# Transformer layer on one core: the order of instructions taken from a time table, queries in six units of 256 and four of 128 per head group

## The chip, the core and the metric

The kernel runs on one core of a Trainium2 chip. A core has five engines, each with its own queue that is worked off strictly in order: TensorE (PE in the profile; its weight loads are shown apart as PEld), VectorE (DVE), ScalarE (ACT), GpSimd (POOL) and SyncE (SP), which here only issues DMAs. Engines meet through semaphores. Matmuls write to PSUM, eight banks of 128 partitions by 512 fp32 values; DVE and ACT read them from there. The metric is the device time of one execution in microseconds (us), lower is better. The kernel before took 1297.13 us (median of three runs, 1290.29 to 1299.14).

## What is computed

A pre-norm attention block and a gated FFN over 2048 tokens of width 512, with 32 heads of 16 columns; inputs and output are bfloat16.

```python
def _A_ref(x, wqkv, wo):            # S = 2048, D = 512, H = 32, Dh = 16
    qkv = (x @ wqkv).reshape(B, S, 3, H, Dh).transpose(2, 0, 3, 1, 4)
    q, k, v = qkv[0], qkv[1], qkv[2]
    scores = jnp.einsum("bhqd,bhkd->bhqk", q, k) * (Dh ** -0.5)
    p = _softmax(scores, axis=-1)
    o = jnp.einsum("bhqk,bhkd->bhqd", p, v)
    return o.transpose(0, 2, 1, 3).reshape(B, S, D) @ wo

def _B_ref(x, w_gate, w_up, w_down):  # F = 1792
    return (_gelu(x @ w_gate) * (x @ w_up)) @ w_down

h = x + _A_ref(_layernorm(x), wqkv, wo)
h2 = h + _B_ref(_layernorm(h), w_gate, w_up, w_down)
```

## The kernel before

**Units.** Heads are taken four at a time, one to each 32-row group of the PE array ("slot": 8 of them). Queries are taken 256 at a time ("group": `gi`, 8 of them). A unit is one group and one slot, so there are 64; a slot's scores for 256 queries are 4 heads x 256 x 2048 numbers.

**Two passes over the scores.** The first pass (`p1_pair`, `p1_consume`) multiplies 128 queries of two heads by 512 keys into two PSUM banks (L653, matmuls in 32-row tiles), and DVE takes the row maxima of both banks in one reduction (L662, 128x1024 in, 128x2 out). A unit has 16 such steps (four key chunks `kc`, two query halves, two pairs of heads), the kernel 1024. GpSimd folds the maxima of the key chunks (L673 to L690), splits the result into three bfloat16 parts (L693 to L696, tile ST), SP transposes them by DMA (L702, tile STG), and GpSimd adds them to spare rows of QT (L707), so that the second pass's matmul already subtracts the maximum. The second pass (`p2_pair`, `p2_consume`) computes the transposed scores, keys on partitions (L728, two matmuls of 256 columns to a bank), and ACT takes exp of a whole bank (L741): 32 banks a unit, 2048 in all. The result goes to a ring of 34 tiles PT. `item_pv` multiplies it by V with a column of ones (L755, four heads in four 32-column tiles), so the denominators come along.

**Rounds.** A loop over ticks (L1150) writes the program. One tick has one first-pass pair, one second-pass pair of an earlier unit (the second pass runs 24 ticks behind), and one piece of "dense" work, the matmuls in whole-array form: projections, V products, output projection (`item_oproj`), gate, up and down of the FFN (`item_gate`, `item_up`, `item_down`). Where no dense piece is ready, `dummy` (L1144) issues filler matmuls of 512 columns. The waits of a tick's row-tiled matmuls are drawn together (`group_begin`, `group_end`). GpSimd's work goes through `PoolStream` with a budget of 1.19 us a tick. Evacuations go to ACT while the first pass lasts (`evac_act`), later to DVE.

```python
cost = dense.piece()
if cost and not p2_started:
    dense.piece()
if (cost or 0) < 2:
    dummy(banks.free[0], 2 - (cost or 0))
run_deferred(tick)
pool.tick()
```

**Start.** SP loads x in four chunks of 512 KB, then wqkv (1536 KB) and wo. DVE takes the statistics of all 16 tiles (L338, L339), GpSimd their rsqrt by a power (L343), DVE normalizes tiles 0 to 11 and GpSimd tiles 12 to 15 (L349); PE transposes (L354), ACT copies out (L356). `w_order` (L361) copies Q's and K's weights into another column order, so that a projection's 128 columns hold the heads of two slots: one in place, one shifted by 16 partitions by a DMA (QKS to QKS2), each then masked. K of head tile 0 for all four key chunks and Q for the first are projected before the first pass starts.

**FFN and tail.** tanh-gelu is put together from five GpSimd operations (L930 to L934) and one ACT tanh (L925). Gate and up work on two blocks of 128 FFN columns for 256 tokens (one bank). The last group's FFN runs after everything else (`tail_a`, `tail_b`), with ACT's own gelu; its layer norm takes row sums from ACT (L1105, L1107) and a chain on GpSimd (L886 to L907).

Of the kernel before, what the change touches and what calls it, by code (L numbers as in the profile page):

```python
# [1 line left out]

# [2 lines left out]

class _Eng:
    def __init__(self, name, sem):
        self.name = name
        self.sem = sem
        self.count = 0  # L10
        self.ops = []
        self.known = {}
        self.group_start = None


class Plan:

    ENGINES = ("pe", "act", "dve", "pool", "sp")

    def __init__(self, nc, es):  # L20
# [10 lines left out]
        self.n_waits = 0  # L31
        self.held = set()
        self.implied = {}

# [6 lines left out]
    def _deps(self, reads, writes):  # L41
        deps = []
        for b in reads:
# [3 lines left out]
            if b in self.held:  # L47
                raise RuntimeError("plan: read of incompletely written buffer %r" % (b,))
# [15 lines left out]
    def _waits_for(self, e, deps, extra=()):  # L64
# [17 lines left out]
        self.n_waits += len(waits)  # L82
        return waits

    def op(self, eng, fn, reads=(), writes=(), sig=True, extra_deps=()):
        e = self.eng[eng]
        deps = self._deps(reads, writes)
        waits = self._waits_for(e, deps, extra_deps)
        if sig:
            e.count += 1  # L90
            tok = (eng, e.count)
        else:
            tok = (eng, e.count + 1)
        if sig:
            self.implied[tok] = dict(e.known)
# [4 lines left out]
    def dma(self, eng, fn, semkey, reads=(), writes=(), extra_deps=()):  # L100
# [3 lines left out]
        waits = self._waits_for(e, deps, extra_deps)  # L104
        self.dma_count[semkey] += 16
        tok = (semkey, self.dma_count[semkey])
        self.implied[tok] = dict(e.known)
# [4 lines left out]
    def group_begin(self, eng):  # L112
        e = self.eng[eng]
        e.group_start = len(e.ops)
        e.group_count = e.count

    def group_end(self, eng):
        e = self.eng[eng]
        i0 = e.group_start
        e.group_start = None  # L120
        if i0 is None or i0 >= len(e.ops):
            return
        allw = []
        for i in range(i0, len(e.ops)):
            fn, waits, sig, dsem = e.ops[i]
            allw.extend(waits)
            e.ops[i] = (fn, [], sig, dsem)
        need = {}
        for (k, v) in allw:
            if k == eng and v > e.group_count:  # L130
                continue
            if v > need.get(k, 0):
                need[k] = v
        fn, _, sig, dsem = e.ops[i0]
        e.ops[i0] = (fn, sorted(need.items(), key=lambda kv: kv[0] != "act"), sig, dsem)

    def wait(self, eng, tokens):
        e = self.eng[eng]
        waits = self._waits_for(e, tokens)
        if waits:  # L140
            e.ops.append((None, waits, False, None))

    def retire(self, keys):
        toks = []
        for b in keys:
            t = self.last_writer.get(b)
            if t is not None:
                toks.append(t)
            toks.extend(self.readers.get(b, ()))
        need = {}  # L150
        for (k, v) in toks:
            if v > need.get(k, 0):
                need[k] = v
        return list(need.items())

    def finish(self, eng="sp"):
        self.wait(eng, [(k, v) for k, v in self.dma_count.items() if v > 0])

    def emit(self, block):
        nc = self.nc  # L160
# [43 lines left out]
NFC = F // 128  # L204
EPS = 1e-5
GC = 0.7978845608028654

NPT_M, NPT_E, NPT_G = 23, 4, 7
NPT = NPT_M + NPT_E + NPT_G
PV_T = (13, 14, 16, 17)  # L210
ADDX = 4
LAGX = 8
PAUSE = 1


def bass_sequential_preLN__mha_block__geglu_ffn__prompt_kernel(nc, A_x, A_wqkv, A_wo, B_x, B_w_gate, B_w_up, B_w_down, out):
    dbg = None
    with ExitStack() as es:
        block = es.enter_context(nc.Block())
        P = Plan(nc, es)  # L220

# [3 lines left out]
        arena = es.enter_context(nc.sbuf_tensor("arena", [128, ARENA // 2], BF16))  # L225
# [26 lines left out]
        wq_r = at("wq_r", [128, 4, D], BF16)  # L252
        wk_r = at("wk_r", [128, 4, D], BF16)
# [977 lines left out]
```

## Time and profile before

| | us |
|---|---|
| median of the runs | 1297.13 |
| profiled execution | 1296.73 |
| its span, first to last instruction | 1294.8 |
| DVE busy | 1198.6 (93%) |
| ACT busy | 1199.7 (93%) |
| PE busy | 1160.2 (90%) |
| POOL busy | 761.0 (59%) |
| first reduction (L662) starts | 35.3 |
| first exponential (L741) starts | 67.6 |
| last reduction ends | 1225.6 |
| last exponential ends | 1258.4 |

The profile is one execution. Busy time is the union of an engine's instructions; matmuls overlap one another, so a busy PE may still be far from full. In the profile's groups each row is a source line with its engine, output and input tiles, shapes and count, then busy time, the mean duration of one in ns, and the idle time of the engine just before, with what ended it. A duration is longer than the distance from one start to the next where an engine overlaps successive instructions; the timeline shows that distance. The granted clock is TensorE's, 1.00 being full speed; over the span its mean was 0.987.

### The profile page before, as it was taken

How to read it: one execution, taken by the hardware profiler on the slowest of the kernel's cores; microseconds unless marked ns; L12 is line 12 of the kernel's file. 1: busy time of each engine (PE TensorE's matmuls, PEld its weight loads, DVE VectorE, ACT ScalarE, POOL GpSimd, SP SyncE). 2: the span in 40 equal slices, each digit the busy share in tenths (PEclk: the TensorE clock that was granted, in tenths of full speed). 3: DMA queues.
4: the chain of work that ended last, by engine and by line, in shares of the span. 5: the costliest groups of instructions: out<-in, count | busy, mean ns of one | idle time of the engine just before them, and what ended most of it. 6: DMA issues, size and time to landing. Idle time of an engine off the chain costs nothing.

```text
span 1294.8 us, 31432 instructions
## 1 busy us (share of the span) xinstructions
PE 1160.2 (90%) x12678; PEld 445.6 (34%) x12678; DVE 1198.6 (93%) x1101; ACT 1199.7 (93%) x2440; POOL 761.0 (59%) x1534
## 2 busy tenths in 40 slices
PE   3999888899998999899999999899998999989998
PEld 2233222333333333333333333233333333333325
DVE  5899999999999999999999999999999999999802
ACT  3599999999999999999999999999999999999972
POOL 5567763387636773477635774467733876367731
PEclk9999999999999999999999999999999999999969
DMA  3110003300010000100010000100001000100000
GB/s 130 42 32 24 20 20 123 81 6 6 5 28 14 6 5 8 34 6 6 4 29 14 6 4 10 26 11 6 6 21 20 6 6 5 28 14 5 6 9 17
DMA packets 48688, 27.45 MB, mean 21 GB/s; under 512 B 34976, under 2 KB 47008, under 8 KB 48544
## 3 DMA queue, kind: packets, MB, share of 16 engines
q1 hardware_dynamic: 48544, 25.44, 7.5%
q8 instruction: 101, 1.65, 0.6%
q14 instruction: 43, 0.35, 0.1%
HBM read 11.80 MB, written 2.10 MB: 11 GB/s over the span
## 4 chain that ended last, share of the span: by engine, by line
DVE 56%; ACT 15%; POOL 15%; PE 11%; issue 2%; DMA 1%; POOLq 0%
DVE PM L662 55%; ACT PTM L741 8%; POOL LINV L790 4%; ACT PTG L741 2%; POOL th_sb L934 2%; PE pbank L728 2%; POOL th_sb L932 2%; PE pbank L1144 2%; PE pbank L942 2%; ACT th_sb L925 2%; PE pbank L653 2%; PE pbank L603 1%; ACT PTE L741 1%; PE pbank L551 1%; POOL QT L707 1%
## 5 line engine op out<-in xcount | busy, mean ns | idle before, releaser
L662 DVE TENSOR_REDUCE PM<-pbank 128x2 f32<-128x1024 f32 x1024 | 1168.4, 1216 | 34.0 <-PE pbank L728 18.2
L741 ACT ACTIVATE PTM<-pbank 128x512 bf16<-128x512 f32 x1388 | 737.9, 661 | 10.4 <-PE pbank L728 4.0
L728 PE MATMUL pbank<-QT,KT 32*128 32x256 bf16 x4096 | 514.0, 275 | 24.1 <-ACT PTM L741 12.8
L653 PE MATMUL pbank<-KT,QT 32*128 32x512 bf16 x2048 | 398.9, 385 | 28.8 <-DVE PM L662 12.8
L1144 PE MATMUL pbank<-ones_bf,ident 128*128 128x512 bf16 x822 | 256.9, 388 | 41.3 <-ACT u_sb L516 7.8
L741 ACT ACTIVATE PTG<-pbank 128x512 bf16<-128x512 f32 x420 | 228.4, 650 | 2.7 <-PE pbank L728 1.3
L653 PEld LDWEIGHTS pbank<-KT,QT 32*128 32x128 bf16 x2048 | 101.5, 91 | 374.2 <-DVE PM L662 148.8
L728 PEld LDWEIGHTS pbank<-QT,KT 32*128 32x128 bf16 x4096 | 172.3, 92 | 89.3 <-ACT PTM L741 47.9
L741 ACT ACTIVATE PTE<-pbank 128x512 bf16<-128x512 f32 x240 | 137.4, 661 | 2.3 <-PE pbank L728 1.3
L755 PE MATMUL pbank<-PTM,VA 128*17 128x256 bf16 x2776 | 126.9, 276 | 1.5
L688 POOL TENSOR_TENSOR MX<-PM,MX 128x8 f32<-128x8 f32 x64 | 12.8, 199 | 170.6 <-DVE PM L662 170.6
L1144 PEld LDWEIGHTS pbank<-ones_bf,ident 128*128 128x128 bf16 x822 | 49.5, 97 | 148.9 <-ACT PTM L741 90.3
L790 POOL TENSOR_TENSOR LINV<-OAT,negone 128x16 f32<-128x16 f32 (+1 forms) x32 | 92.7, 2896 | 11.8 <-DVE OAT L505 11.8
L677 POOL TENSOR_TENSOR MX<-PM,MX 128x8 f32<-128x8 f32 x64 | 12.9, 202 | 108.8 <-DVE PM L662 108.8
L755 PEld LDWEIGHTS pbank<-PTM,VA 128*17 128x17 bf16 x2776 | 60.6, 90 | 45.9 <-issue 29.3
L942 PE MATMUL pbank<-hnT_l,wu_sb 128*128 128x256 bf16 x448 | 69.2, 281 | 4.7 <-ACT PTG L741 0.2
L942 PE MATMUL pbank<-hnT_l,wg_sb 128*128 128x256 bf16 x448 | 67.9, 277 | 4.2 <-ACT PTM L741 0.6
L934 POOL TENSOR_TENSOR th_sb<-th_sb,g_sb 128x512 f32<-128x512 f32 x49 | 62.0, 1266 | 4.1
L707 POOL TENSOR_TENSOR QT<-QT,STG 128x256 bf16<-128x256 bf16 x64 | 42.7, 667 | 36.9 <-DMA STG<-ST 36.9
L931 POOL TENSOR_TENSOR th_sb<-th_sb,g_sb 128x512 f32<-128x512 f32 x49 | 62.0, 1266 | 2.9
L983 POOL TENSOR_TENSOR GUT<-th_sb,u_sb 128x512 bf16<-128x512 f32 x49 | 62.1, 1268 | 2.7
L990 PE MATMUL pbank<-wd_sb,GUT 128*128 128x512 bf16 x224 | 61.3, 386 | 0.5
(128 smaller groups left out, 1073.0 us busy)
## 6 DMA issues: line engine op xcount, KB each, us to landing
QKS<-QKS SPq DMA_DIRECT2D x32, 112.0 KB, 2.1
x_sb<-in_A_x_dram SPq DMA_DIRECT2D x4, 512.0 KB, 5.5
xres<-in_A_x_dram SPq DMA_DIRECT2D x16, 128.0 KB, 2.2
out_dram<-out_sb SPq DMA_DIRECT2D x16, 128.0 KB, 1.8
wg_sb<-in_B_w_gate_dram SPq DMA_DIRECT2D x4, 448.0 KB, 5.1
wu_sb<-in_B_w_up_dram SPq DMA_DIRECT2D x4, 448.0 KB, 4.9
wqkv_sb<-in_A_wqkv_dram SPq DMA_DIRECT2D x1, 1536.0 KB, 10.3
wd_sb<-in_B_w_down_dram SPq DMA_DIRECT2D x3, 512.0 KB, 6.2
```

The costliest lines, as they stand in the source:

```text
L653: P.op("pe", lambda e, g=g, b=b: e.matmul(pbank[:, b, :], QT[32 * g:32 * g + 32, c, slot, 128 * qt:128 * qt + 128], KT[32 * g:32 * g + 32, ...
L662: P.op("dve", lambda e: e.tensor_reduce(out=PM[:, par, qt, kc, g:g + 2], in_=pbank[:, b:b + 2, :], axis=AX.X, op=ALU.max), reads=[("pb", b ...
L728: P.op("pe", lambda e, g=g, b=b, kt=kt, i=i: e.matmul(pbank[:, b, 256 * i:256 * i + 256], KT[32 * g:32 * g + 32, slot, 128 * kt:128 * kt + ...
L741: P.op("act", lambda e, b=b, pi=pi: e.activation(out=PTt(pi), in_=pbank[:, b, :], func=ACT.Exp), reads=[("pb", b)], writes=[("PT", pi)], e ...
L755: P.op("pe", lambda e, g=g, kt=kt, pi=pi, i=i: e.matmul(pbank[32 * g:32 * g + 17, b, 0:256], VA[:, kt, 4 * slot + g, :], PTt(pi)[:, 256 * ...
L790: P.op("pool", lambda e: e.tensor_tensor(out=li, in0=oat4[:, :, :, 16], in1=negone[:, 0:8 * ns].rearrange("p (q h) -> p q h", q=2), op=ALU ...
L931: o(1.27, lambda e: e.tensor_tensor(out=ts_, in0=ts_, in1=gs, op=ALU.mult), [("th", par), ("g", par)])], then=done)
L934: o(1.27, lambda e: e.tensor_tensor(out=ts_, in0=ts_, in1=gs, op=ALU.mult), [("th", par), ("g", par)])], then=lambda: defer(1, lambda: lat ...
L942: P.op("pe", lambda e, dc=dc, fc=fc, i=i: e.matmul(pbank[:, b, 256 * i:256 * i + 256], w[:, dc, 128 * fc:128 * fc + 128], hT[:, dc, :], st ...
L983: P.op("pool", lambda e: e.tensor_tensor(out=o_ap, in0=shp(ts_), in1=shp(us), op=ALU.mult), reads=[("th", par), ("u", par)], writes=o_keys ...
L990: P.op("pe", lambda e: e.matmul(pbank[:, b, :], GUT[:, fc, 128 * k:128 * k + 128], wd_sb[:, fc, :], start=(fc == 0), stop=False), reads=[( ...
L1144: P.op("pe", lambda e: e.matmul(pbank[:, b, :], ident[:], ones_bf[:, 0:512], start=True, stop=True), reads=["ident", "ones_bf"], writes=[( ...
```

## The change

The whole scheduling half of the kernel is rewritten; the operations on the data stay mostly the same.

- **Groups.** 2048 queries are six groups of 256 and four of 128, so 80 units. In a 128-query unit the second pass puts four matmuls of 128 columns in a bank, gate and up put four blocks of FFN columns in a bank. There the maxima of the four key chunks are folded by one small DVE reduction (`negm_small`); in the last unit DVE does the splitting and the addition too.
- **Order.** `Plan` keeps a modelled time for every instruction. The main loop compares when the next first-pass pair, the next second-pass bank and the next dense piece could start, and writes out the one that comes first by its rules; GpSimd's jobs have priorities, extra ACT passes wait for a gap of two exponentials. There are no ticks and no grouped waits. Fillers of 256 columns are written where nothing could start within 0.35 us by the table.
- **First units.** The first-pass steps of units 0 and 1 alternate by key chunk. Only K and Q of head tile 0 for the first 512 tokens are projected ahead; the other chunks follow between the reductions. Statistics of tiles 8 to 15 are taken by two ACT passes each, and GpSimd normalizes these tiles.
- **Transfers.** The first four tiles of x are loaded one by one, then K's columns of wqkv, Q's, the rest of x, V's.
- **Weights.** Q's and K's weights are used in their own column order; V's columns are picked by `head(slot, g)`, and the transposed output is written back in the right order.
- **Tail.** The last group has 128 queries; its layer norm takes statistics straight from PSUM on DVE, in two halves.

```diff
+GROUPS = [(256 * i, 256) for i in range(6)] + [(1536 + 128 * i, 128) for i in range(4)]
...
+    def mm(self, fn, reads=(), writes=(), n=512, mode="f", tile=0, sig=False, slow=1, extra=()):
...
+        run = slow * n / 2400.0 + 0.0025
+        if mode == "f":
+            run = max(run, 0.058)
...
-        for c in range(NCH):
-            P.dma("sp", lambda e, c=c: e.dma_start(out=x_sb[:, 4 * c:4 * c + 4, :], in_=xv[:, 4 * c:4 * c + 4, :]),
-                  ("x", c), writes=[("x", c)])
-        P.dma("sp", lambda e: e.dma_start(out=wqkv_sb[:], in_=wv), "wqkv", writes=["wqkv"])
+        for t in range(4):
+            P.dma("sp", lambda e, t=t: e.dma_start(out=x_sb[:, t, :], in_=xv[:, t, :]), ("x", t), writes=[("x", t)], lat=2.4 + 0.1 * t, ivl=0.4)
+        P.dma("sp", lambda e: e.dma_start(out=wqkv_sb[:, :, D:2 * D], in_=wv[:, :, D:2 * D]), "wk", writes=["wk"], lat=3.8)
+        P.dma("sp", lambda e: e.dma_start(out=wqkv_sb[:, :, 0:D], in_=wv[:, :, 0:D]), "wq", writes=["wq"], lat=4.8)
...
+        def head(slot, g):
+            return 8 * (slot // 2) + 2 * g + slot % 2
...
+        for kc in range(4):
+            for ui in (0, 1):
+                seq += [(ui,) + s_ for s_ in steps_of(ui) if s_[0] == kc]
+        for ui in range(2, NU):
+            seq += [(ui,) + s_ for s_ in steps_of(ui)]
...
+        def negm_small(ui):
+            par = ui % 2
+            last = ui == NU - 1
+            dve(lambda e: e.tensor_reduce(out=NEGM[:, par, 0:4], in_=PM[:, par, :, 0, :].rearrange("p k g -> p g k"), axis=AX.X, op=ALU.max, negate=True),
+                [("PM", par, k_, 0, gp_) for k_ in range(4) for gp_ in range(2)], [("NEGM", par)], 0.1, 0.2)
...
+            P.dma("sp", lambda e: e.dma_start_transpose(out=STG[:, par, 0:w].rearrange("p (q s) -> p q s", q=nq), in_=ST[:, par, 0:nq].rearrange("p q s -> p (q s)")),
+                  ("stT", par), reads=[("ST", par)], writes=[("STG", par)], lat=2.35, ivl=0.1)
...
+        def pool_bank():
+            best, bt = None, INF
+            for b in (2, 3, 4, 5, 6, 7) if p1_over[0] else (4, 5, 6, 7):
...
+            for i in range(nk):
+                kt = m * nk + i
+                P.mm(lambda e, kt=kt, i=i: e.matmul(pbank[:, b, w * i:w * i + w], KT[32 * g:32 * g + 32, slot, 128 * kt:128 * kt + 128],
+                                                    QT[32 * g:32 * g + 32, c, slot, col:col + w], start=True, stop=True, tile_position=(32 * g, 0)),
...
+        def late_stats(c):
+            sl = slice(4 * c, 4 * c + 4)
+            for t in range(4 * c, 4 * c + 4):
+                for (func, dst, key) in ((ACT.Copy, hsum, "hs1"), (ACT.Square, hsq, "hq1")):
+                    def go(t=t, func=func, dst=dst, key=key):
+                        act(lambda e: e.activation(out=PTM[:, t, :], in_=x_sb[:, t, :], func=func, accum_out=dst[:, t:t + 1]), [("x", t)], [(key, t), ("PT", t)], 512, ivl=0.9, lat=1.0)
...
-            if (cost or 0) < 2:
-                dummy(banks.free[0], 2 - (cost or 0))
...
+            if P.pe_mode == "r" and best_row <= tr + 0.06:
+                kind = "row"
+            elif sd < INF and ed + 0.09 <= min(D1, D2) + 0.03 and sd <= best_row + 0.5:
+                kind = "dense"
+            elif best_row < INF and best_row <= sd + 0.3:
+                kind = "row"
+            elif sd < INF:
+                kind = "dense"
+            else:
+                kind = None
...
+            if best_row > P.pe_at("f") + 0.35:
+                b, bt = pool_bank()
+                if b is not None and bt <= P.pe_at("f") + 0.02:
+                    dummy(b, 256)
+                    continue
+            if f1 <= f2 + 0.02:
+                p1_issue()
+            else:
+                p2_issue(tl, b2)
```

## The prediction

> **What bounds the kernel now.** I first cut the span into stretches at the first reduction, the first exponential, the last reduction and the last exponential, and read the busy time of each engine there (columns: stretch, its length, busy us and instructions of each engine, granted clock, DMA):
>
> ```profile
> 0.00:35.30 35.30, 14.97 (x86) 8.73 (x86) 18.18 (x55) 14.14 (x24) 16.48 (x32) 1.00 0.36 120
> 35.30:67.60 32.30, 31.27 (x150) 9.82 (x150) 29.59 (x25) 16.24 (x30) 20.42 (x34) 1.00 0.16 46
> 67.60:1225.60 1158.00, 1052.62 (x11997) 398.92 (x11996) 1138.81 (x1000) 1135.17 (x2327) 705.78 (x1437) 1.00 0.07 18
> 1225.60:1258.40 32.80, 31.09 (x254) 9.35 (x253) 1.97 (x4) 25.83 (x50) 13.69 (x18) 0.67 0.04 11
> 1258.40:1294.80 36.40, 30.29 (x203) 18.74 (x194) 10.03 (x18) 8.27 (x15) 4.58 (x13) 0.92 0.04 15
> ```
>
> The third busy figure is DVE, the fourth ACT. Between the ends both run at 98%; before 35.30 and after 1225.60 DVE has little to do. The groups say what the 98% is, the timeline how fast a reduction can follow another:
>
> ```profile
> L662 DVE TENSOR_REDUCE PM<-pbank 128x2 f32<-128x1024 f32 x1024 | 1168.4, 1216 | 34.0 <-PE pbank L728 18.2
> L1144 PE MATMUL pbank<-ones_bf,ident 128*128 128x512 bf16 x822 | 256.9, 388 | 41.3 <-ACT u_sb L516 7.8
> ```
>
> ```profile
> 699.33 5.74 DVE L662 TENSOR_REDUCE PM<-pbank 128x2 f32<-128x1024 f32 x5
> 700.14 2.11 ACT L741 ACTIVATE PTM<-pbank 128x512 bf16<-128x512 f32 x4
> ```
>
> Five reductions in 5.74 us, the last 1.214 long: one starts every 1.131 us. Four exponentials in 2.11 us, the last 0.66: every 0.48 (0.477 between most starts in the trace). So 1024 reductions need 1023 x 1.131 + 1.214 = 1158.2 us of DVE, and 2048 exponentials 977 us of ACT, to which some 140 us of evacuations, tanh and squares come. DVE is the floor, ACT some 4% below it in issue time. The middle holds 1000 reductions in 1158.0 us, 27 us over their 1131. The chain of waits at the end:
>
> ```profile
> 1241.59 0.54 PE pbank L728 x4
> 1242.13 0.96 PE pbank L1144 x2
> 1243.10 0.54 PE pbank L728 x4
> ...
> 1269.60 0.40 PE pbank L1078 x4
> ...
> 1271.71 6.49 PE pbank L942 x48
> ```
>
> At the lower clock (0.67 in this stretch) a round for two exponentials takes 1.51 us; then come the last FFN's 256 queries. The profiled execution took 1296.73 us, 1.93 around its span, and lies 0.4 under the median of the runs.
>
> **The change, part by part.** The 1024 reductions and 2048 exponentials of the same size stay: nothing in the floor moves. All gain must come from the ends and the 27 us.
>
> *Head.* x comes first as four tiles of 128 KB. Four issues took 2.11 us, 0.53 each; a load of that size landed after 2.2 (the xres row), so tile 0 is there at 0.79 + 2.2 = 3.0, not 4.88. Statistics take 0.8 a tile (4.88 to 5.70). Then per tile: next statistics 0.8, an addition 0.16, GpSimd's power 0.58 (the rows of 128x1), normalizing 0.40, handovers: 2.0. Tile 3 ends at 3.0 + 0.8 + 3 x 2.0 + 1.2 = 11.0. Transposes 0.4, their copy 0.6, the K projection 1.0, its evacuation 0.8: 13.8, and Q's evacuation on DVE 14.8. The built order puts four normalizations (1.15 each with their powers) and two statistics ahead of the first reduction on DVE: 14.8 + 6.2 = 21. PE has 16 V-projection matmuls and eight transposes before the first pair (to about 18), which that covers; the V weights, now tenth in SP's queue, must be there by 14: before, the same 3.5 MB of x and weights had landed by 2.94 + 10.3 = 13.2, so they just are. The eight weight reorderings (0.29 each on DVE) go, since the head permutation moves into V's columns and a strided transpose output. First reduction at 21 instead of 35.3, between 18 and 26.
>
> Tiles 8 to 15 get their statistics on ACT: sixteen passes at about 0.6 each, ten us, in a stretch where ACT was busy 16 of 32 us; then eight normalizations on GpSimd at 0.77. By the built order their eighth pass stands behind about 17 us of ACT work, so chunk 2 of K comes at about 40, and the two interleaved units consume 16 reductions, 18 us, from 21 on: to 39. Chunk 3 comes at about 50, when chunk 2 is used up at 49. I take 6 us for these waits (0 to 12). Were the two units not interleaved, only 8 reductions would cover them. The first exponential stands behind 34 pairs instead of 25, at about 66, as before; ACT's 977 + 140 from there fits.
>
> *Middle.* Here the fixed rounds with two filler matmuls give way to an order written out from a time table. By the built order PE changes between its tile modes 1522 times instead of 2097 (about 0.1 us each: 58 us of PE), and 822 fillers (0.22 each: 180 us) become 230, nearly all at the ends. The lag of exponentials behind reductions stays (975 against 974 at reduction 512). The 27 us went mostly to reductions behind L728 (18.2), which waited for banks that ACT held while it waited for GpSimd's gelu; the new order emits a tanh only where its product should be there. I take half of the 27, 13.5, and keep none (0) and all (27) as ends.
>
> The last 512 queries come in units of 128: 31 small maxima on DVE at 0.1, 3 us; for a quarter of the reductions, 256, PE's score and V matmuls double in number at half the width. What a 128-column matmul costs is in the last transposes: four in 0.40 us, one 0.22 to 0.23 long by its own row, so 56 ns each, weight loads included. Per reduction PE then has 8 transposed-score matmuls, 2 rounds of four V matmuls, and 1.75 of gate and up, 11.75 x 56 = 0.66, plus 0.08 for the rest of the FFN and 0.16 for 1.6 mode changes: 0.90, and 1.12 if the first scores' 0.22 hides nowhere. That is under 1.131, but close; 3 us for it.
>
> *End.* After the last pair of scores 52 exponentials stand on ACT (before: 50): 24.8, and 2.8 for tanh and evacuations, less 2 since that pair is issued ahead of its reduction, plus 3 for PE: 28.6, against 32.8. The chain of the last unit (its maximum and splitting on DVE 0.9, SP's transpose 2.3, addition 0.25) is covered by the 20 exponentials of the unit before, 9.5. From the last exponential on, 36.4 now: the FFN of one 128-row tile is 112 x 56 + 28 x 107 = 9.3 instead of 19.5, and statistics straight from PSUM on DVE (2.5) stand in for two ACT passes and GpSimd's chain (6.6 from 1263.02). 36.4 - 10.2 - 4.1 = 22.1, and 2 less for half-width steps: 20 (17 to 26).
>
> Sum: 21 + 1158.2 + 3 + 6 + 13.5 + 3 + 28.6 + 20 + 1.9 = 1255.
>
> **Rivals.** *PE becomes the bound in the narrow units* (slower than before). 11.75 matmuls at c, 0.24 beside: DVE's 1.131 is passed at c = 75 ns if the first scores are hidden, at 57 if not. If each 128-column matmul waits for its whole weight load (92 to 98 ns by their rows, 94 taken), a reduction needs 1.35 to 1.57 of PE, 55 to 110 us over 256: 1310 to 1365. Against it is the 56 ns of the four transposes, four in a row only; for it, that such a stream stands nowhere else in the profile. The Trainium skill ("TensorE: Matmul & The Clock Gate", Back-to-back issue gap) gives about 81 ns for streams of load and matmul at N=128; by it the sum would be 1272, or 1327 with nothing hidden. The trace's 56 differs from it. Chance 0.13.
>
> *The clock falls in the middle.* The fillers were a seventh of PE's streaming time there. Without them the dense work fills 25% and both score streams 19% (all overlapped) to 57% (none). In the trace the stretches of 3.4 us before the two falls in the middle (at 752 and 1161 us) stream 45% and 38%; the leanest without a fall 44%. Exponentials free banks one by one, so the scores hardly all overlap; I expect 60 to 70%. At half clock a round costs 0.38 more (1.51 - 1.131): a fifth of the rounds, 78 us, 1333. Chance 0.05. The same page (Part 1) lets the clock fall after an idle window of about 3.4 us; by that rule there would be no fall here, but the fourth stretch above shows 0.67 with PE busy 31 of 33 us.
>
> *The written order waits.* An engine can't pass over a step that the time table had too early. The table gives SP 0.1 us for issuing a transpose; the row of L702 has 1.17, landing 2.3 to 4.1. If each of the 80 units held up PE by half a us, 40 us: 1295. Against: a unit's exponentials begin some 8 reductions, 9 us, after its last one, and the chain takes 5 to 8. Chance 0.10.
>
> *Only the ends gain, or all waits go* (1268 or 1241) are inside my case, chance 0.72; the built order shows the change doing what it says.
>
> **The numbers.** Likeliest 1255. My case with all ends low is 18 + 1158 + 3 + 0 + 0 + 3 + 27 + 17 + 2 = 1228, seldom all at once: low 1232. High 1290 takes in most of the third rival and the mild part of the first. This kernel's runs tell about 1% from no change: 1284 and 1310. Faster: 0.71 of my case, 0.04 of the first rival, 0.02 of the third: 0.77. Same: 0.01 + 0.04 + 0.05 = 0.10. Slower: 0.05 + 0.05 + 0.03 = 0.13.
>
> **What would show it.** First reduction at 18 to 26 us; reductions still 1.131 apart; DVE idle in the middle under 25 us; PE's clock 1.00 there; no denser waits of DVE for PE in the last quarter; under 24 us after the last exponential. Wrong if DVE's idle time grows after reduction 768 (first rival), if half-clock windows stand in the middle (second), or if DVE waits recur at unit starts (third).

## The result, and the profile after

The changed kernel took 1379.65 us (median of four runs, 1365.37 to 1385.21), the kernel before on the same chip 1296.04. The ratio is 1.0634, with a 95% interval of 1.0545 to 1.0723: slower by some 83 us, where 42 us less had been forecast. The profiled execution took 1379.94 us, its span 1378.2. The ratios of the experiments below leave out single runs that took longer than the others of their kernel, for a cause that isn't known: 1378.08 of a_share3000 (the profiled one, so no small difference is read from its row), 1412.33 of a_wide, 2582.0 of a_noint and 1639.63 of the kernel before.

The same cut as before, at the first reduction (23.00), the first exponential (76.20), the last reduction (1323.90) and the last exponential (1352.20). Columns again: stretch, its length, busy us and instructions of PE, PEld, DVE, ACT, POOL, granted clock, DMA share, GB/s.

```profile
0.00:23.00 23.00, 21.50 (x116) 10.16 (x117) 11.73 (x36) 11.34 (x22) 7.92 (x22) 1.00 0.61 193
23.00:76.20 53.20, 46.95 (x256) 18.34 (x253) 38.10 (x35) 28.92 (x63) 42.75 (x63) 0.90 0.09 26
76.20:1323.90 1247.70, 1180.49 (x13188) 508.08 (x13190) 1147.70 (x1022) 1135.69 (x2351) 703.07 (x1391) 0.80 0.07 17
1323.90:1352.20 28.30, 26.21 (x582) 19.56 (x570) 7.22 (x20) 27.21 (x57) 21.85 (x24) 0.94 0.05 13
1352.20:1378.20 26.00, 22.83 (x248) 17.36 (x248) 6.74 (x17) 6.38 (x13) 4.94 (x8) 0.99 0.04 11
```

Both ends are about where the forecast had them: the first reduction at 23.0 instead of 35.3, and 54.3 us from the last reduction to the end instead of 69.2. Most of the loss is in the third line (the second is 20.9 us longer, too, with 35 DVE instructions instead of 25). The third has nearly the same work for DVE and ACT as before (1148 and 1136 us, against 1139 and 1135), takes 90 us more for it, and its clock is 0.80 where it was 1.00. The row of the granted clock, one digit for a fortieth of the span, shows that this is no single event:

```profile
PEclk9899766697957889689885889778976689988879
```

Summed up from the records of the clock, of which the last ends 2 us behind the span, 507.7 us ran at half clock, in 50 separate falls of 2.6 to 27.3 us; before it was 36.5 us, most of it after the last reduction. The groups of the two score passes and of the fillers (busy us, mean ns, then the engine's idle time before them and what ended it), and what DVE waited for (total us, times, longest):

```profile
L684 DVE TENSOR_REDUCE PM<-pbank 128x2 f32<-128x1024 f32 x1024 | 1185.0, 1215 | 115.1 <-PE pbank L822 60.9 <-PE pbank L681 50.9
L681 PE MATMUL pbank<-KT,QT 32*128 32x512 bf16 x2048 | 502.3, 455 | 17.7 <-DVE PM L684 13.9
L440 PE MATMUL pbank<-ones_bf 128*128 128x256 bf16 (+1 forms) x230 | 48.4, 335 | 1.8 <-POOL ones_bf L467 1.4
```

```profile
DVE PM L684 <- PE pbank L822: 60.9, 130, 1.9
DVE PM L684 <- PE pbank L681: 50.9, 67, 5.3
```

A reduction is as long as it was (1215 ns against 1216), but 115 us of idle time stand before the reductions instead of 34, and it is PE that ends it. No single wait is long: 130 of 1.9 us or less, 67 of 5.3 or less. That is PE running a little behind DVE again and again. PE's score matmuls went from 385 ns on average to 455.

To see whether the clock and the waits belong together I put each distance between two reduction starts down to the clock it ran at, and took off the 1.131 us that a reduction needs. At full clock 639 distances have a mean of 1.159 and 18.2 us of waits in all, 28 ns each; 1017 such distances had 27.9 us before, 27 ns each. The 384 distances that ran at half clock in part or whole have 124.5 us: 300 wholly at half clock with a mean of 1.459, 98.5 us, and 84 mixed ones, 26.0.

### The profile page after: what moved, and what is told of

Its sections match the earlier page's. It is cut to its first block, busy times and chain, and to the rows that moved or that the text cites. A ratio compares the mean times of both kernels' runs of the same rounds, so it can differ in the third digit from the quotient of the medians.

```text
span 1378.2 us, 34328 instructions
## 1 busy us (share of the span) xinstructions
PE 1298.0 (94%) x14370; PEld 573.5 (42%) x14370; DVE 1211.5 (88%) x1127; ACT 1209.5 (88%) x2503; POOL 780.5 (57%) x1505
## 4 chain that ended last, share of the span: by engine, by line
ACT 44%; PE 41%; DVE 6%; POOL 5%; issue 2%; DMA 2%; SPq 0%; POOLq 0%; ACTq 0%; DVEq 0%
ACT PTM L831 24%; PE pbank L822 15%; ACT PTG L831 8%; PE pbank L681 8%; PE pbank L853 7%; DVE PM L684 6%; ACT PTE L831 5%; PE pbank L1029 4%; PE pbank L1057 3%; PE pbank L954 1%; ACT th_sb L1010 1%; ACT g_sb L540 1%; ACT u_sb L540 1%; PE pbank L639 1%; ACT QKS L622 1%
## 5 line engine op out<-in xcount | busy, mean ns | idle before, releaser
L684 DVE TENSOR_REDUCE PM<-pbank 128x2 f32<-128x1024 f32 x1024 | 1185.0, 1215 | 115.1 <-PE pbank L822 60.9
L831 ACT ACTIVATE PTM<-pbank 128x512 bf16<-128x512 f32 x1388 | 739.8, 694 | 69.2 <-PE pbank L822 66.9
L822 PE MATMUL pbank<-QT,KT 32*128 32x256 bf16 (+1 forms) x5120 | 698.2, 287 | 29.0 <-ACT PTM L831 6.0
L681 PE MATMUL pbank<-KT,QT 32*128 32x512 bf16 x2048 | 502.3, 455 | 17.7 <-DVE PM L684 13.9
L822 PEld LDWEIGHTS pbank<-QT,KT 32*128 32x128 bf16 x5120 | 268.3, 99 | 308.7 <-ACT PTM L831 162.7
L853 PE MATMUL pbank<-PTM,VA 128*17 128x256 bf16 (+1 forms) x3470 | 162.8, 295 | 2.0 <-ACT PTM L831 0.5
L887 POOL TENSOR_TENSOR LINV<-OAT,negone 128x8 f32<-128x8 f32 (+1 forms) x78 | 109.4, 1410 | 26.3 <-ACT OAT L540 17.0
L853 PEld LDWEIGHTS pbank<-PTM,VA 128*17 128x17 bf16 x3470 | 75.6, 99 | 68.7 <-issue 42.8
L1029 PE MATMUL pbank<-hnT_l,wu_sb 128*128 128x256 bf16 (+1 forms) x504 | 75.5, 290 | 5.2 <-ACT g_sb L540 2.6
L1029 PE MATMUL pbank<-hnT_l,wg_sb 128*128 128x256 bf16 (+1 forms) x504 | 70.6, 279 | 10.3 <-issue 5.9
L1057 PE MATMUL pbank<-wd_sb,GUT 128*128 128x512 bf16 (+1 forms) x238 | 73.6, 408 | 0.6
L1001 POOL TENSOR_TENSOR GUT<-th_sb,u_sb 128x512 bf16<-128x512 f32 (+1 forms) x54 | 66.7, 1237 | 3.1
L1016 POOL TENSOR_TENSOR th_sb<-th_sb,g_sb 128x512 f32<-128x512 f32 (+1 forms) x54 | 66.7, 1236 | 1.9
L1012 POOL TENSOR_TENSOR th_sb<-th_sb,g_sb 128x512 f32<-128x512 f32 (+1 forms) x54 | 66.7, 1235 | 1.9
L1014 POOL TENSOR_TENSOR th_sb<-g_sb 128x512 f32<-128x512 f32 (+1 forms) x54 | 54.8, 1015 | 14.8 <-ACT g_sb L540 13.0
L1011 POOL TENSOR_SCALAR th_sb<-th_sb 128x512 f32<-128x512 f32 (+1 forms) x54 | 32.7, 605 | 50.8 <-ACT th_sb L1010 50.6
```

The source lines that it names most:

```text
L681: P.mm(lambda e, g=g, b=b0 + jj: e.matmul(pbank[:, b, :], QT[32 * g:32 * g + 32, c, slot, col:col + 128], KT[32 * g:32 * g + 32, slot, 512 ...
L684: dve(lambda e: e.tensor_reduce(out=PM[:, par, kc, qh, 2 * gp:2 * gp + 2], in_=pbank[:, b0:b0 + 2, :], axis=AX.X, op=ALU.max), [("pb", b0) ...
L822: P.mm(lambda e, kt=kt, i=i: e.matmul(pbank[:, b, w * i:w * i + w], KT[32 * g:32 * g + 32, slot, 128 * kt:128 * kt + 128], QT[32 * g:32 * ...
L831: act(lambda e: e.activation(out=PTt(pi), in_=pbank[:, b, :], func=ACT.Exp), [("pb", b)], [("PT", pi)], 512, lat=0.605, ivl=0.48, extra=dX)
L853: P.mm(lambda e, g=g, kt=kt, pi=pi, i=i: e.matmul(pbank[32 * g:32 * g + 17, b, 0:w], VA[:, kt, head(slot, g), :], PTt(pi)[:, w * i:w * i + ...
L887: inv = [((lambda e, a=a: e.tensor_tensor(out=LINV[:, par, a:a + hh], in0=oat[:, a:a + hh, 16], in1=negone[:, 0:hh], op=ALU.pow)), [("OAT" ...
```

## The experiments

The table has all runs. "Waits" are the time between first and last reduction beyond the 1158.2 us that DVE needs, split by the clock; the columns "to last exp" and "to end" are the stretches behind the last reduction and the last exponential. All but the median and the ratio come from the one profiled execution. Each ratio is against runs of the kernel before on the same chip, whose medians were 1296.04 to 1298.87; "half clock" is the sum over the clock's records, in us.

| run | median us | ratio, 95% interval | half clock | first reduction | waits, full clock | waits, half or mixed | to last exp | to end |
|---|---|---|---|---|---|---|---|---|
| before | 1296.04 | 1 | 36.5 | 35.3 | 27.9 | 4.2 | 32.8 | 36.4 |
| changed kernel | 1379.65 | 1.0634 (1.0545-1.0723) | 507.7 | 23.0 | 18.2 | 124.5 | 28.3 | 26.0 |
| b_nofill | 1355.59 | 1.0439 (1.0411-1.0467) | 494.7 | 34.7 | 10.1 | 83.5 | 30.3 | 35.7 |
| b_fill66 | 1347.26 | 1.0377 (1.0346-1.0409) | 239.1 | 35.2 | 19.1 | 69.8 | 32.8 | 35.2 |
| a_fill20 | 1390.22 | 1.0708 (1.0669-1.0748) | 445.8 | 23.3 | 16.2 | 118.6 | 29.3 | 39.5 |
| a_force | 1355.10 | 1.0454 (1.0403-1.0504) | 281.0 | 23.9 | 24.8 | 80.3 | 25.6 | 41.7 |
| a_mult | 1386.53 | 1.0707 (1.0650-1.0763) | 513.2 | 23.6 | 20.4 | 105.7 | 26.6 | 50.2 |
| a_wide | 1396.12 | 1.0742 (1.0687-1.0798) | 504.0 | 22.8 | 15.9 | 117.5 | 28.6 | 44.4 |
| a_share3000 | 1368.06 | 1.0517 (1.0463-1.0570) | 186.2 | 22.5 | 16.5 | 68.7 | 70.9 | 39.5 |
| a_ms3000 | 1355.05 | 1.0452 (1.0408-1.0497) | 129.7 | 23.4 | 24.6 | 36.2 | 64.6 | 48.7 |
| t_2200_74 | 1367.39 | 1.0574 (1.0527-1.0621) | 179.1 | 22.4 | 28.2 | 48.7 | 43.8 | 54.1 |
| a_noint | 1405.34 | 1.0835 (1.0791-1.0879) | 531.5 | 23.4 | 14.8 | 150.9 | 29.8 | 22.1 |
| b_head | 1297.15 | 1.0002 (0.9980-1.0024) | 34.1 | 31.7 | 30.2 | 4.2 | 32.4 | 35.5 |
| b_head2 | 1295.51 | 0.9996 (0.9977-1.0016) | 57.1 | 32.7 | 27.5 | 11.1 | 30.3 | 36.3 |

Names that begin with b are edits of the kernel before, the others of the changed kernel. The profiled execution of t_2200_74 was the fastest of its four (1357.17).

**Is it the fillers? The old order without them.** b_nofill takes the 822 fillers out of the kernel before and nothing else:

```diff
-            if (cost or 0) < 2:
-                dummy(banks.free[0], 2 - (cost or 0))
```

> The kernel before, with its 822 filler matmuls left out and nothing else changed. Clock theory (the fillers held TensorE's clock up, and their loss is what made the changed kernel slow): half-clock stretches over a quarter to a half of the span, mean clock 0.75 to 0.90, 1340 to 1400 us. Order theory (the written order's waits made it slow, the low clock is only seen along with them): the rounds are untouched, so the clock stays above 0.95 and the time between 1280 and 1300 us.

It came out 57 us slower than before (1298.87 on that chip), though PE has some 180 us less to stream (822 at 0.22). The clock row, the reductions, and the stretch from the first exponential to the last reduction:

```profile
PEclk9988865788788787788788887887877887878759
...
L662 DVE TENSOR_REDUCE PM<-pbank 128x2 f32<-128x1024 f32 x1024 | 1181.5, 1217 | 81.9 <-PE pbank L728 64.4 <-PE pbank L653 12.9
```

```profile
66.90:1286.40 1219.50, 1018.57 (x11192) 394.80 (x11190) 1151.98 (x1000) 1143.13 (x2326) 706.53 (x1437) 0.81 0.07 17
```

The old order shows the changed kernel's picture: 0.81 in the middle, 495 us at half clock, waits of DVE for PE. Nothing else of the change is in this kernel, so the fillers alone carry that much here: useless for the output, they held the clock up. The order theory's 1280 to 1300 us is out.

**What about a filler holds the clock? The same streaming on a quarter of the array.** b_fill66 keeps all 822 fillers and their 512 columns, but lets them use 66 rows and 66 columns of the array:

```diff
-                P.op("pe", lambda e: e.matmul(pbank[:, b, :], ident[:], ones_bf[:, 0:512], start=True, stop=True),
+                P.op("pe", lambda e: e.matmul(pbank[0:66, b, :], ident[0:66, 0:66], ones_bf[0:66, 0:512], start=True, stop=True),
```

> The kernel before, with every filler cut to 66 rows and 66 columns of the array: 512 columns streamed as before, in the same mode, over 27% of the array. If the clock goes by how long matmuls stream: as before, clock about 0.98, 1290 to 1300 us. If it goes by how much of the array works: most of the fillers' effect is gone, clock 0.75 to 0.92, 1330 to 1390 us.

```profile
PEclk9999999889798987999898987999878988989869
...
L1144 PE MATMUL pbank<-ones_bf,ident 66*66 66x512 bf16 x822 | 289.0, 430 | 32.5 <-ACT u_sb L516 6.4 <-ACT PTM L741 6.4 <-ACT OA L516 1.6
```

PE streams as many columns as in the kernel before, and still 239 us fall to half clock: 1347.26. So the time for which PE streams isn't all that the clock goes by. I also cut the full-clock time, from 23 us on, into windows of 3.41 us along the clock's own records and counted in each the share of the time in which matmuls stream, and the streamed columns weighted by the share of the 128 x 128 cells that the matmul uses (32 rows by 128 columns for the scores, 128 by 17 for the V products; fp32 transposes, one each 109 ns, count twice). Windows with 50 to 65% of streaming time never fell in the kernel before (0 of 112); in b_fill66 17 of 111 did, and in the changed kernel 34 of 77. By the weighted count, windows that stay at full clock have a median of 0.45 in the changed kernel, those before a fall 0.28; in b_fill66 it is 0.41 and 0.25. By streaming time alone it is 0.71 and 0.57 in the changed kernel. The weighted count tells the two kinds apart better there (of a hundred pairs, one window of each kind, it has 98 in the right order, streaming time 91; in b_fill66 99 and 96), but not in b_nofill (95 and 97). That is a correlation, and it gives no sharp threshold: in the changed kernel windows up to 0.38 fell, and from 0.29 on some stayed.

**Fillers put back into the written order.** a_fill20 only lowers the gap from which the new order fills (as many columns as 275 fillers of 512; the changed kernel has 145, the kernel before 822); a_force fills up to 1024 columns of whole-array or V work before each first-pass pair (429).

```diff
 a_fill20
-            if best_row > P.pe_at("f") + 0.35:
+            if best_row > P.pe_at("f") + 0.20:
 a_force
...
+                if p2_on[0] and not p1_over[0]:
+                    want = 1024 - since[0]
+                    b, bt = pool_bank()
+                    while want > 0 and b is not None and bt <= P.pe_at("f") + 0.05:
+                        dummy(b, min(512, want))
+                        want -= 512
+                    since[0] = 0
```

> The changed kernel, with fillers written where nothing can start within 0.20 us instead of 0.35: 260 fillers of 256 columns more, 28 us of streaming, some 15% of what the kernel before had. Clock theory: the half-clock time falls from 508 us to 300 to 450, and the time with it, by 0.3 us for each 1.45 us: 1335 to 1370 us. Order theory: more for PE to do and nothing gained, 1375 to 1395 us.

> The changed kernel, with fillers in front of a first-pass pair until some 1024 columns of whole-array or column-tiled work have been written since the pair before, as in the rounds of the kernel before (178 fillers of 512 columns, 53 of 489, 107 of 256 and 120 of 8 more). Clock theory: half-clock time under 150 us, 1260 to 1310 us. Order theory: PE has more work on the path, 1380 us or more.

a_fill20 is a miss for the clock theory's time, and its total is the one that the order theory gave: 62 us less at half clock, waits down by only 8, and 13.5 us more behind the last exponential; its interval overlaps the changed kernel's. a_force is a hit for the clock theory in direction only, and outside the numbers of both (under 150 us of half clock and 1260 to 1310, or 1380 and more): 227 us less at half clock, waits down by 38, and the time by 25, since 16 us came back at the end. Its first 128 reductions still took 165.7 us (the changed kernel 165.2, before 149.9), so that stretch has a cause of its own, too.

**GpSimd's form, and the narrow units.** The new table plans 0.74 us for a normalization of 128x512 on GpSimd written as (x - mean) * rstd. a_mult writes it as x * rstd + nmr, as the kernel before did, with two small multiplications more per call; a_wide takes the last 512 queries as one group of 256 and two of 128.

```diff
 a_mult
-                    ops.append(o(lambda e, t=t: e.tensor_scalar(out=xn_sb[:, t, :], in0=x_sb[:, t, :], scalar1=mv[:, t, 0:1], scalar2=rstd[:, t:t + 1], op0=ALU.subtract, op1=ALU.mult),
+                    ops.append(o(lambda e, t=t: e.tensor_scalar(out=xn_sb[:, t, :], in0=x_sb[:, t, :], scalar1=rstd[:, t:t + 1], scalar2=nmr2[:, t:t + 1], op0=ALU.mult, op1=ALU.add),
...
 a_wide
-GROUPS = [(256 * i, 256) for i in range(6)] + [(1536 + 128 * i, 128) for i in range(4)]
+GROUPS = [(256 * i, 256) for i in range(7)] + [(1792 + 128 * i, 128) for i in range(2)]
```

> Changed kernel with GpSimd normalizing as x*rstd + nmr (mult, add) in place of (x - mean)*rstd (subtract, mult), two small multiplications more per call. Plan-error theory: the 128x512 normalizations take 0.77 us instead of 2.08, so the 23 of them come as the time table has them; the first 128 reductions shorten from 165 us by 5 to 12, later units little: 1360 to 1375. Clock theory: apart from that early part nothing changes, half-clock time stays at 450 to 520 us and the rest of the span at its length. If the wrong GpSimd durations were what threw the whole written order out of step: under 1340, with DVE's waits between first and last reduction under 90 us.

> Changed kernel with the last 512 queries as one unit group of 256 and two of 128 (instead of four of 128). Narrow-unit theory (PE bound in 128-query units): 128 fewer narrow reductions save 12 to 25 us, 1350 to 1367. Clock theory: half-clock time is spread over the whole span, so 1370 to 1385, half-clock time 480 to 520 us. If narrow units only cost clock (more short matmuls), the half-clock time of the seventh group's stretch falls and about 3 to 8 us go.

The operation itself, in the changed kernel and then in a_mult:

```profile
L1247 POOL TENSOR_SCALAR xn_sb<-x_sb,mv,rstd 128x512 bf16<-128x512 bf16 x8 | 16.5, 2078 | 0.1
...
L978 POOL TENSOR_SCALAR OnT<-xres,mv,rstd 128x512 bf16<-128x512 bf16 x15 | 31.4, 2096 | 1.3
```

```profile
L1252 POOL TENSOR_SCALAR xn_sb<-x_sb,rstd,nmr 128x512 bf16<-128x512 bf16 x8 | 6.0, 769 | 0.0
```

2.08 us against 0.77 for the same tile. In the changed kernel's chain of waits the late chunks of K hang on it (start, length, what):

```profile
35.17 4.14 POOL xn_sb L1247 x2
...
40.11 2.08 POOL xn_sb L1247
42.24 0.61 PE pbank L502 x4
...
50.89 6.21 POOL xn_sb L1247 x3
57.15 0.61 PE pbank L502 x4
```

Normalizing one chunk of four tiles takes 8.3 us instead of 3.1, and PE's transposes for the chunk start right behind. With the other form the first exponential comes at 69.4 instead of 76.2 and the first 128 reductions take 159.2 us instead of 165.2, as the plan-error theory had it; the half-clock time stayed (513.2), as the clock theory had it. The total was forecast at 1360 to 1375 and came out at 1386.53: the 17 us less of waits were lost behind the last exponential (50.2 instead of 26.0). There the profile has whole FFN pieces that the changed order had done earlier: GpSimd is busy 25.28 us of that stretch, against 4.94. The order is one written plan, and a small edit moves what it leaves for the end.

a_wide speaks against the narrow units as the cause. Half of the narrow reductions gone, half-clock time the same, waits down by 9 us only (133.4 against 142.7); a loss to the end of 18 us took more than that. Its total also lies above the 1370 to 1385 that the clock theory gave, by that end.

**Enough fillers for the clock.** a_share3000 fills wherever fewer than 3000 whole-array columns were streamed in the last 3.0 us (the columns of 910 fillers of 512); a_ms3000 is the same with GpSimd's (mult, add) form (924).

```diff
...
+            if p2_on[0] and not p1_over[0] and best_row > tr + 0.06 and sum(c_ for _, c_ in dense_log) < 3000:
+                b, bt = pool_bank()
+                if b is not None and bt <= P.pe_at("f") + 0.05:
+                    n_ = [n for n in (512, 256, 128) if P.pe_at("f") + n / 2400.0 + 0.09 <= min(D1, D2) + 0.03]
+                    if n_:
+                        dense_log.append((P.pe_last, n_[0]))
+                        dummy(b, n_[0])
+                        continue
```

> Changed kernel with whole-array filler matmuls wherever fewer than 3000 whole-array columns were streamed in the last 3.0 us and the next score or V matmul is not due yet (about 194 us of fillers instead of 31; more tile-mode changes, about 2120 instead of 1500). Clock theory: granted clock above 0.95, half-clock time under 120 us, and since the old kernel lost 57 us for 495 us of half clock, the time falls by 40 to 60 us: 1320 to 1340. Order theory (the loss lies in the written order's waits, and PE at half clock would be hidden in a kernel that waits anyway): half-clock time falls as much, but the time stays at 1360 or more, and the waits of DVE for the score matmuls stay above 100 us at full clock.

> Both: the fillers by share and GpSimd's (mult, add) form. Clock theory with the plan-error term: 10 to 15 us below the run with the share fillers alone, 1305 to 1330, and if the rest of the written order costs nothing at full clock, with head and tail of the change kept, 1270 to 1290, under the kernel before. Order theory: 1350 or more.

The stretches of a_ms3000 from its first exponential (69.80), last reduction (1242.30) and last exponential (1306.90):

```profile
69.80:1242.30 1172.50, 1137.24 (x13474) 494.91 (x13473) 1133.82 (x1021) 1097.17 (x2252) 641.93 (x1361) 0.95 0.07 18
1242.30:1306.90 64.60, 59.74 (x1200) 41.58 (x1200) 14.63 (x36) 61.20 (x127) 46.56 (x59) 0.87 0.08 13
1306.90:1355.60 48.70, 45.56 (x489) 36.81 (x489) 9.25 (x21) 10.54 (x20) 23.74 (x28) 1.00 0.03 9
```

For the reductions the clock theory is borne out. The middle's clock is 0.95, DVE's waits fall from 142.7 to 60.8 us, and the last reduction ends 82 us earlier than in the changed kernel, with the table's rules as they were. The totals, 1368 and 1355, are those of the order theory all the same (1360 or more, 1350 or more), and the clock theory's 1320 to 1340 and 1305 to 1330 were missed. But the order theory's reason isn't there: it wanted over 100 us of waits at full clock, and there are 16.5 and 24.6. The gain was given back behind the last reduction, where 127 ACT instructions stand instead of 57. Counted from the starts, the exponentials were 61 behind the reductions (two per reduction) when the 128th started, 83 at the 512th and 115 at the last; in the changed kernel it was 47 to 55 at the same three. Then the late FFN pieces follow. Against the kernel before, a_ms3000 is 12 us ahead at the first reduction, and then loses 29 in waits, 32 up to the last exponential and 12 behind it.

**Is that lead only a choice of the order?** t_2200_74 holds score pairs back once they are more than 74 ahead, and fills to 2200 columns:

```diff
+            if f2 < INF and 2 * p1_i[0] - exps[0] > 74:
+                f1 = max(f1, f2 + 0.05)
...
```

> Changed kernel with GpSimd's (mult, add) form, whole-array fillers up to 2200 columns in 3.0 us, and score pairs held back once their reductions stand more than 74 half-reductions ahead of the exponentials. With 3000 columns and nothing held back the lead of the scores grew from 61 to 115 exponentials and the last ones ran out 65 us after the last reduction. If that lead was only the order's choice, the time moves back into the rounds and the total falls to 1310 to 1330 (half-clock time about 150 us, last exponential within 45 us of the last reduction). If the fillers take banks and tile-mode changes that the exponentials needed (the loss is given back wherever it is put), the end comes nearer but the reductions stand further apart and the total stays at 1345 to 1370.

This kernel puts other values into a part of its output, by a step that isn't known; it issues the same 1024 reductions and 2048 exponentials, and only its time is used. Against a_ms3000 the stretch behind the last reduction shrank by 21 us, the waits grew by 16 and the end by 5; the two profiled executions took the same time (1357.17 and 1357.38). The median is 1367.39, the second theory (1345 to 1370). In both versions most of what the clock gains is given back, though they differ in the columns as well as in the hold. Why wasn't settled. Fillers take one of the four PSUM banks of the second pass, and by the built order PE changes its tile mode 2092 times here and 1476 times in a_mult; which of the two counts wasn't tried.

**The interleaving.** a_noint runs the first two units one after the other:

```diff
-        for kc in range(4):
-            for ui in (0, 1):
-                seq += [(ui,) + s_ for s_ in steps_of(ui) if s_[0] == kc]
-        for ui in range(2, NU):
+        for ui in range(NU):
```

> Changed kernel with its first two units one after the other instead of interleaved by key chunk. By the prediction's term the interleaving covers the late K chunks: without it the first 128 reductions take 8 to 15 us more than 165, since only eight reductions per chunk stand before each wait, and the first exponential comes 10 to 15 us before 76. If the waits for K chunks are what sets this stretch in both orders, the reductions of unit 1 only move and the first 128 take the same within 4 us. Clock theory: half-clock time after that as in the changed kernel, 450 to 520 us; total 1375 to 1400.

```profile
38.08 6.21 POOL xn_sb L1244 x3
...
50.87 8.27 POOL xn_sb L1244 x4
59.14 0.05 issue
59.19 0.61 PE pbank L502 x4
```

Its lines stand three higher (L1244 is the normalization). The chunks of K are as late (their normalizations end at 44.3 and 59.1, in the changed kernel at 42.2 and 57.1), and fewer reductions stand before each wait: the first 128 take 182.5 us instead of 165.2. So the interleaving is worth 17 us, a little more than the 8 to 15 expected. The first exponential, expected 10 to 15 us earlier, came at 75.8, as in the changed kernel (76.2): it waits for the last chunk, not for the other unit.

**A head gain in the old order.** b_head moves three steps in the kernel before: the weight reorderings ahead of the last statistics, Q of the first chunk right behind its K, and the fourth chunk's normalization behind four projections. The transposes of that chunk then overwrite banks from which three of the early projections are copied once more later, so the second slot's heads of two key chunks and the first query chunk hold other data, at the same work. b_head2 also leaves out the fillers behind the last pair of scores.

```diff
 b_head
-        ln1_stats(3)
-        ln1_norm(2, "dve")
-        w_order(wk_r, D, "wk_r")
-        ln1_norm(3, "pool")
-        w_order(wq_r, 0, "wq_r")
+        w_order(wk_r, D, "wk_r")
+        w_order(wq_r, 0, "wq_r")
+        ln1_norm(2, "dve")
+        ln1_stats(3)
...
-        ks = [(item_projT, "k", 0, c) for c in range(NCH)] + [(item_projT, "q", 0, 0)]
+        ks = [(item_projT, "k", 0, 0), (item_projT, "q", 0, 0)] + [(item_projT, "k", 0, c) for c in range(1, NCH)]
...
-        dense.run_items(5)
+        dense.run_items(4)
+        ln1_norm(3, "pool")
...
+        dense.run_items(1)
 b_head2
-            if (cost or 0) < 2:
+            if (cost or 0) < 2 and p1_ok:
```

> Kernel before with an earlier head only: weight reorderings ahead of the last statistics, K and Q of the first chunk projected before the fourth chunk is normalized and transposed. The first reduction comes at 30 to 32 us instead of 35.3; the rounds behind it, their fillers and the clock stay as they are (half-clock time under 60 us). If a head gain reaches the end in the old order, 3 to 5 us: ratio 0.996 to 0.998; if the rounds simply wait for the later K chunks, 1.000.

> The same, and no fillers once the last pair of scores has been issued. Clock theory: rounds of two exponentials there are already at half clock (1.51 us each, of which 0.96 is two fillers), so without them a round is bound by ACT at about 1.0 and the stretch from the last reduction to the last exponential falls from 32.8 to 28 to 30 us; what follows it may start at half clock and give 2 us back. Total 4 to 8 us under the kernel before: ratio 0.994 to 0.997.

```profile
0.00:31.70 31.70, 13.29 (x85) 8.06 (x86) 18.32 (x56) 12.92 (x22) 16.37 (x32) 1.00 0.38 133
31.70:66.50 34.80, 32.34 (x147) 10.02 (x150) 29.56 (x25) 17.15 (x31) 20.52 (x35) 0.95 0.15 42
```

3.6 us at the first reduction are 1.1 at the first exponential (67.6 before) and nothing in the runs: 1.0002 (0.998 to 1.0024). The second stretch got 2.5 us longer where the first got 3.6 shorter. In b_head2 the stretch behind the last reduction fell to 30.3 (28 to 30 expected), and the total shows nothing of the 4 to 8 us expected: 0.9996. Neither is a version to keep.

## Why the prediction was wrong

By its own terms, with the profiled execution's values: 23.0 (forecast 21) + 1158.2 + 142.7 of waits (25.5 as the sum of 3, 6, 13.5 and 3) + 28.3 (28.6) + 26.0 (20) + 1.7 = 1379.9. The waits are 117 of the 125 us by which it missed.

**The step that failed is the second rival's chance of 0.05.** The mechanism was in the text, with its price: 0.38 us more for a round at half clock, a fifth of the rounds, 1333. The price was near: 0.328 us over the floor, measured as 1.459 - 1.131. The share was 38% of the distances (384 of 1023), not a fifth, and 0.72 of the chance lay on a case whose 13.5 us for the middle were reckoned at full clock. The argument was that falls come after stretches with 38% and 45% of streaming time and that the new order would stream 60 to 70%. The second half held (a median of 0.71 in windows that keep the clock), the first didn't: half of the windows before a fall stream 57% or more. Two falls in the old profile were taken for the threshold, in a kernel whose fillers hide where it lies. And streaming time alone was too little of a measure: the fillers use the whole array, a score matmul a quarter of it and a V matmul an eighth (17 columns of 128). By time the fillers were 15 of the 66% that PE streamed in the old middle, which is more than a fifth of the streaming and not a seventh; by cells they were more still. The old profile had the hint: weighted by cells, the windows before its two falls have 0.30 and 0.25, the lowest of its middle, where the leanest that stayed has 0.31. b_fill66 shows that whole-array work counts for more than its time, b_nofill that taking it out costs 57 us without anything else of the change.

The prediction set a page's rule beside this, the Trainium skill's "TensorE: Matmul & The Clock Gate" (Part 1), by which the clock falls after an idle window of 3.4 us. The trace disagrees as to the cause: in the 3.4 us before a fall the longest time without a matmul had a median of 0.2 us in the changed kernel and was never over 1.6, but for the last fall, as the program ends (2.5). It agrees as to the grid: 49 of the 50 falls last a whole multiple of 3.41 us. The same page's section "A second HAM failure mode: psum-queue depth-cycling" tells of a clock that goes back and forth through frequent short idling, which is nearer; b_fill66, with the same streaming as before, 203 us more at half clock and falls after windows with 50 to 65% of streaming time, from which none came before, shows that idling alone isn't it either.

**The rest of the middle.** At full clock the written order waits as long as the old one (18.2 us in 639 distances, 28 ns each; before 27), so the half of the old 27 us that the sum took off isn't there, a matter of some 14 us: at this rate all 1023 distances have 29. The third rival, steps that come too early in the order, doesn't show in DVE's waits. It shows elsewhere: what the plan leaves for the end moved by up to 28 us between runs that differ little (22.1 to 50.2 without the share fillers).

**Early waits, 6 us (0 to 12).** The first 128 reductions waited 20.4. With GpSimd's (mult, add) form they waited 14.3, with that and the clock held (a_ms3000) 9.0, inside the range. So the term left out two causes: 6 us for an operation priced at 0.77 by a row with other arithmetic, and about 5 that went with the clock. The interleaving itself did what was said.

**Narrow units.** The first rival's sign, denser waits after reduction 768, is hardly there: 0.153 us per reduction in the last quarter, 0.130 in the 640 before it, and at full clock 4.8 us in 161 distances. The 56 ns that it hung on held, for 96 matmuls in the tail's chain with their weight loads, 5.36 us or 55.8 ns each:

```profile
1365.70 5.36 PE pbank L1157 x96
```

The Trainium skill's figure for such a stream (same page, Back-to-back issue gap, about 81 ns) doesn't hold for this row, and the sum by it would have been 1271, not 1272. At half clock the narrow units do cost more, 0.377 over the floor against 0.316.

**Head and end.** The first reduction came at 23.0, inside 18 to 26, and by the path that the sum had. The V weights landed at 15.86, not by 14, and the first pair waited for the V projections, but it was done by 20.1; DVE was what came last:

```profile
15.81 0.75 DVE L613 TENSOR_SCALAR QT<-pbank,qmask 128x512 bf16<-128x512 f32 x1 [2.64 <-PE pbank L588]
...
22.25 0.87 DVE L492 TENSOR_SCALAR xn_sb<-x_sb,mv,rstd 128x512 bf16<-128x512 bf16 x1 [0.65 <-POOL rstd L489]
23.04 1.20 DVE L684 TENSOR_REDUCE PM<-pbank 128x2 f32<-128x1024 f32 x1
```

Q's evacuation ended at 16.6 instead of 14.8, and the normalizations and statistics behind it took 6.5 instead of 6.2. From the last reduction on, 28.3 was as forecast. After the last exponential it took 26.0, the edge of 17 to 26: the FFN was 9.7 us as reckoned, but rests of the unit before and its GpSimd chain stood first. Both ends together brought 27 us. With the 384 distances of the half clock at 28 ns, too, the sum would come to 1266, but no run shows such a kernel: with the clock held, a_ms3000 took 1355.

**What stays open:** whether this order could have its fillers without paying elsewhere, and so how much of the 83 us is the clock's alone. No version tried came under the kernel before.

## What to carry over

Work that only fills an engine may hold its clock, so an edit that removes it must be priced at the lower clock first, and the cheapest test is to remove the filler alone. Two events are no threshold; where a profile hardly shows a state, its chance can't be put at 0.05 by an argument from what it does show. A table of durations for a written order has to be measured operation by operation, arithmetic included, and what the order leaves behind the last critical step needs a bound of its own.

## What the hardware showed that I hadn't expected

- The granted clock goes with how much of the array works, and not with streaming time alone: with fillers on 66 x 66 of it, half-clock time rose from 36.5 to 239.1 us, and without fillers to 494.7.
- GpSimd's two-step operation on 128x512 bfloat16 took 2.08 to 2.10 us as (subtract, mult) and 0.77 as (mult, add), 23 operations of each.
